# One-hots of a routing table moved to VectorE, more row tiles, and another order of expert passes

## The chip, the cores and the metric

The kernel runs on one core of a Trainium2 chip. The metric is the device time of one execution in microseconds (us); lower is better. Engines are called PE (TensorE, matrix products), PEld (its weight loads), DVE (VectorE), ACT (ScalarE), POOL (GpSimd) and SP (SyncE, which here only issues DMAs). Each engine works through its own queue in order.

## The reference

Two blocks follow each other, all in float32.

The first is a gated linear recurrence over 768 tokens, for 4 sequences of 8 heads with 48 channels. With f = sigmoid(f_logit), for each token

```
state = f[:, :, t, :, None] * state + k[:, :, t] (outer) v[:, :, t]
y[:, :, t] = q[:, :, t] @ state
```

The result, seen as 3072 tokens of 384 values, enters a mixture of experts. A token picks the best of 4 groups, then the best of 4 experts in that group (argmax of a softmax each), so that one of 16 experts works on it:

```
h = maximum(x @ w1[g, e], 0)        # 384 -> 1024
out[token] = g_w * e_w * (h @ w2[g, e])   # 1024 -> 384
```

An expert's two weight matrices are 1.5 MB each.

## The kernel before

**The recurrence stage.** Tokens are worked on in 6 chunks of 128, and a chunk in two halves of two sequences, which makes 12 units. Every unit passes through five stages, each one a generator: `gated`, `turned`, `scored`, `weighed`, `done`. In iteration i unit i is gated, unit i-1 turned, and so on. The text string `WEAVE` gives the order in which the generators of an iteration take one step each (a letter for a stage), and `LATE` does that for the last two iterations. On PE one unit is, in this order: `y` of the old state (L539), the logits `lT` (L574), `y` of the new scores (L544), scores `ap` (L523), the transpose `x_ps` (L582), `tr_q`/`tr_k` (L501), the state update `ds` (L554), `cs` (L479).

**Routing.** When both halves of a chunk are `done`, the generator `route` takes its 128x4 tokens through argmax (DVE), a rank within the expert (`rk`, two kinds of matmul, L191 and L194), a slot number `atf` (L207), weights, and last the table of slots: for each of the chunk's four groups of 128 tokens, `b`, POOL makes a one-hot `ln` of the slot's lane (L225) and a one-hot `val` of the slot's block times the two digits of the token's number (L228, two instructions). PE multiplies them into `tb` (L233, four matmuls that add up in one bank), and DVE adds that to `table` (L234). The letter `r` in the weave takes a step of it, only in iterations where the unit routed is the second half of its chunk; all of its steps stand in the last part of the iteration.

**Early experts.** After chunk 3 (`CLOSE`) `choose_early` takes the two fullest experts, loads their weights, and `early()` runs one block of 128 of their tokens each, in the last two iterations (letter `e`).

**The main stage.** `choose` ranks the experts by size and makes `who` (expert of each place) and `rows_p` (token numbers of each slot). Then come 16 passes, one for each place: the two early experts have a second block of 128, the others a width from `WIDTHS` (230 down to 174). A pass is: `fetch`, POOL's gather of token rows by indirect DMA (L355, one for 128 rows); `turn_in`, transposes (L368); `up` (L378); `down` (L404, or L397 for a block of 128, whose result is by token already); for the others `turn_out`, transposes back (L413); `put`, a scaling on DVE (L388) and a scatter by indirect DMA (L389). Row tiles of the early experts and of passes 0 and 1 come from a pool with two buffers; those of the other passes from one with four. Weights sit in three buffers: two in the pool `wp`, one in `wq`. Weights for pass n+3 are asked for after `down` of pass n.

**What sets the order.** The kernel is written with a framework that plans each engine's queue from the written order and from its own estimate of when operands and buffers are ready; a later instruction can be put ahead of one that it expects to be late. It adds all waits. At the end every engine reads two flags (L766) and branches over a slow path that isn't taken here.

Of the kernel before, what the change touches and what calls it, by code (L numbers as in the profile page):

```python
# [22 lines left out]
def kernel(  # L23
# [141 lines left out]
    def route(c, lg, sb, tabled=True):  # L165
# [53 lines left out]
        nc.sync.dma_start(out=rows_of(c)[:, :, DM:RW], in_=meta)  # L219
        yield  # L220
        if tabled:
            pairs = []
            for b in range(B):
                ln = tmp([P, P], "ln", BF16, bufs=4)
                nc.gpsimd.tensor_scalar(ln, lanes, atf[:, b, 0:1], None, OP.is_equal)  # L225
                val = tmp([P, 2, GE, 2], "val", BF16, bufs=4)
                for m in range(2):
                    nc.gpsimd.tensor_scalar(val[:, m], heads_of, atf[:, b, 1:2], part[:, c, b, m:m + 1], OP.is_equal, OP.mult)  # L228
                pairs.append((ln, val))
            yield  # L230
            tb = bank([P, 2, GE, 2], "tb")
            for b, (ln, val) in enumerate(pairs):
                nc.tensor.matmul(tb.rearrange("p m e j -> p (m e j)"), lhsT=ln, rhs=val.rearrange("p m e j -> p (m e j)"), start=(b == 0), stop=(b == B - 1))  # L233
            nc.vector.tensor_tensor(table, table, tb, OP.add)  # L234
        yield

# [113 lines left out]
    def fetch(pool, rows, n, top=N):  # L350

        w = {"n": n, "pool": pool, "blocks": [(j, min(P, n - j * P)) for j in range((n + P - 1) // P)]}
        w["x"] = pool.tile([P, len(w["blocks"]), RW], FP32, tag="xg", bufs=2 if pool is ep else 4, name="xg")
        for j, m in w["blocks"]:
            nc.gpsimd.indirect_dma_start(out=w["x"][0:m, j, :], out_offset=None, in_=x_dram[0:1 + top, :], in_offset=bass.IndirectOffsetOnAxis(ap=rows[0:m, j:j + 1], axis=0))  # L355
        return w
# [75 lines left out]
    with ExitStack() as fast:  # L432
# [132 lines left out]
        def done(i):  # L565
            c, s = units[i]
            xT = live[i]["xT"]
            if s == 0:
                groups[c] = sb.tile([P, B, NL], FP32, tag="lgs", name="lgs")

            lT = bank([P, P], "lT")
            for a in range(HP):
                for r in range(2):
                    nc.tensor.matmul(lT[DP * r:DP * r + DP, :], lhsT=gw[:, 2 * a + r].rearrange("p s l -> p (s l)"), rhs=xT[:, r, a, :], start=(a == 0), stop=(a == HP - 1), skip_group_check=True)  # L574
            lgT = sb.tile([P, P], FP32, tag="lgT", name="lgT")
            nc.scalar.copy(lgT, lT)
# [16 lines left out]
        def routed(i):  # L593

            c, s = units[i]
            if s:
                yield from route(c, groups[c], sb)
                if c == CLOSE:
                    choose_early(sb)
                    for p in range(EARLY):  # L600
                        weights[p] = load_weights(wp, who[0:1, p:p + 1])
                    first.append(early())
                    next(first[0])
                    yield

        first = []
        restart()
        WEAVE = "w d w s d t w d g s d t g r t r g r t r g r t r r".split()
        LATE = "w d w d d r e r d r e r e r r e r r e r e r".split()
        STAGES = (("g", gated), ("t", turned), ("s", scored), ("w", weighed), ("d", done), ("r", routed))  # L610
        LATER = dict(g=0, t=1, s=2, w=3, d=4, r=4)
        load(0)
        for i in range(NU + 4):
# [6 lines left out]
            gens = {nm: fn(i - LATER[nm]) for nm, fn in STAGES if 0 <= i - LATER[nm] < NU}  # L620
            for nm in WEAVE if i < NU + 2 else LATE:
                if nm in gens:
                    next(gens[nm], None)
                elif nm == "e":
                    next(first[0], None)

    with tc.tile_pool(name="cb", bufs=1) as cb:
        choose(cb)
# [2 lines left out]
    main = ctx.enter_context(ExitStack())  # L631
    wq = main.enter_context(tc.tile_pool(name="wq", bufs=1))
    mo = main.enter_context(tc.tile_pool(name="mo", bufs=2))
    NP = GE + EARLY

    def pass_of(n):

        if n < EARLY:
            return n, fetch(ep, rows_p[:, n, 1:2], P)
        p = n  # L640
        return p, fetch(mo, rows_p[:, p, :], WIDTHS[p - EARLY])

    fari = const([1, 1], I32, "fari")

# [11 lines left out]
    ws = {}  # L656
    for n in range(3):
        ws[n] = pass_of(n)[1]
    weights[2] = load_weights(wq, who[0:1, 2:3])
    for _ in first[0]:  # L660
        pass

    def run_up(n):
        for _ in up(ws[n], weights[n][0]):
            pass

    turn_in(ws[0])
# [1 line left out]
    turn_in(ws[1])  # L669
    for n in range(GE):  # L670
        if n + 3 < GE:
            ws[n + 3] = pass_of(n + 3)[1]
# [6 lines left out]
        down(ws[n], weights.pop(n)[1])  # L679
# [78 lines left out]
        beyond(True, sb)  # L758


    both = const([1, 2], I32, "both_i")
    rest = const([1, 1], I32, "rest")
    nc.vector.tensor_copy(both[:, 0:1], fari)
    nc.vector.tensor_scalar(rest, b_end, 0, None, OP.is_gt)
    nc.vector.tensor_tensor(both[:, 1:2], fari, rest, OP.max)
# [55 lines left out]
```

## Time and profile before

| what | value |
|---|---|
| median of 3 runs | 565.67 us (564.66 to 568.5) |
| profiled execution, its own time | 564.0 us |
| its span (first to last instruction) | 561.8 us |
| mean granted clock of PE | 0.91 of full |
| PE busy | 470.8 us, 84% of the span, 3855 instructions |
| DVE busy | 169.5 us, 30% |
| ACT busy | 115.8 us, 21% |
| POOL busy | 114.4 us, 20% |
| moved by DMA | 84.61 MB, 151 GB/s in the mean |

The profile is of one execution. Busy shares are means over stages that differ, so they say which engine does most, and not what a stage waits for. The recurrence stage lasts until about 241 us; the stretch to 265 us holds the choice of experts and the start of the main stage.

### The profile page before, as it was taken

The page shows a single profiled execution, that of the slowest core. Times are in us where ns is not written, and L with a number is a line of the kernel's source. Part 1 is how long each engine was busy: PE and PEld are TensorE (multiplying, and loading weights), DVE is VectorE, ACT ScalarE, POOL GpSimd, SP SyncE. Part 2 cuts the span into 40 slices and gives each one's busy share as a digit, 9 for nine tenths or more (in the row PEclk, how much of TensorE's full clock was granted, in tenths as well). Part 3 has the DMA queues.
Part 4 walks back from the last instruction along what each step waited for, and adds up shares of the span by engine and source line. Part 5 has one row for each costly group of instructions (what it writes and reads, how often), then busy time and mean ns, then how long its engine had stood idle before and what let it go on. Part 6 is the DMA issues. An engine that isn't in the chain of part 4 may idle for free. (4 is left out here: it accounts for less than half of the span.)

```text
span 561.8 us, 9341 instructions
## 1 busy us (share of the span) xinstructions
PE 470.8 (84%) x3855; PEld 422.7 (75%) x3855; DVE 169.5 (30%) x435; ACT 115.8 (21%) x245; POOL 114.4 (20%) x197
## 2 busy tenths in 40 slices
PE   2689689597795958781999999979999979999990
PEld 0468568386683847740988999979999879999990
DVE  4435626346155341363111122022111210221110
ACT  3466616255242211100100000101001000001000
POOL 5000130400404121246000012221222222122121
PEclk9789979689696877977899999999999998999996
DMA  9798746637201950138355257537655673574010
GB/s 192 122 212 192 158 91 153 131 83 158 45 29 30 345 190 29 30 116 247 127 194 208 94 225 257 169 112 262 220 174 175 240 255 86 194 256 154 7 38 24
DMA packets 138677, 84.61 MB, mean 151 GB/s; under 512 B 110629, under 2 KB 130131, under 8 KB 138627
## 3 DMA queue, kind: packets, MB, share of 16 engines
q1 hardware_dynamic: 132610, 74.07, 45.7%
q0 software_dynamic: 6016, 9.87, 5.7%
q8 instruction: 32, 0.52, 0.4%
q14 instruction: 19, 0.15, 0.1%
HBM read 74.38 MB, written 9.83 MB: 150 GB/s over the span
## 5 line engine op out<-in xcount | busy, mean ns | idle before, releaser
L378 PE MATMUL hp<-xe,w 128*128 128x128 f32 (+14 forms) x864 | 140.1, 323 | 1.6 <-DVE xe L369 1.6
L378 PEld LDWEIGHTS hp<-xe,w 128*128 128x128 f32 x864 | 137.0, 193 | 3.3 <-DVE xe L369 2.5
L404 PE MATMUL yo<-h,w 128*128 128x230 f32 (+13 forms) x672 | 118.5, 337 | 0.0
L404 PEld LDWEIGHTS yo<-h,w 128*128 128x128 f32 x672 | 114.7, 192 | 0.5
L389 POOL DMA_INDIRECT out_dram<-yt,xg x32 | 34.7, 1083 | 196.0 <-DVE yt L388 142.8
L380 DVE TENSOR_SCALAR h<-hp 128x256 f32<-128x256 f32 (+14 forms) x36 | 19.5, 541 | 146.9 <-PE hp L378 146.9
L225 POOL TENSOR_SCALAR ln<-lanes,atf 128x128 bf16<-128x128 f32 x24 | 14.4, 599 | 191.9 <-DVE atf L207 191.9
L382 ACT ACTIVATE h<-hp 128x256 f32<-128x256 f32 (+14 forms) x36 | 17.2, 478 | 140.7 <-PE hp L378 140.7
L525 DVE TENSOR_TENSOR am<-ap,tri 128x512 f32<-128x512 f32 x48 | 30.9, 684 | 43.4 <-PE ap L523 43.4
L355 POOL DMA_INDIRECT xg<-x_dram,rows_p x30 | 33.2, 1106 | 49.3 <-issue 36.0
L405 ACT COPY yT<-yo 128x230 f32<-128x230 f32 (+13 forms) x28 | 9.1, 326 | 156.3 <-PE yo L404 156.3
L479 PE MATMUL cs<-ld_f,tri 128*128 128x384 f32 x48 | 23.0, 570 | 15.6 <-ACT ld_f L473 15.6
L233 PE MATMUL tb<-val,ln 128*128 128x64 bf16 x24 | 5.1, 211 | 36.3 <-POOL val L228 36.3
L368 PE MATMUL xg_ps<-ident,xg 128*128 128x128 f32 (+14 forms) x96 | 13.5, 264 | 19.0 <-DMA xg<-x_dram,rows_p 18.8
L539 PEld LDWEIGHTS y<-Tq,st 48*64 48x64 f32 x320 | 16.4, 174 | 16.2 <-issue 16.1
L523 PE MATMUL ap<-Tq,Tk 48*128 48x128 f32 x384 | 28.2, 287 | 0.0
L544 PE MATMUL y<-am,v 128*64 128x128 f32 x384 | 27.1, 302 | 0.0
L368 PEld LDWEIGHTS xg_ps<-ident,xg 128*128 128x128 f32 (+14 forms) x96 | 10.4, 143 | 22.0 <-issue 11.9
L523 PEld LDWEIGHTS ap<-Tq,Tk 48*128 48x128 f32 x384 | 23.6, 190 | 4.1 <-issue 3.9
L544 PEld LDWEIGHTS y<-am,v 128*64 128x64 f32 x384 | 25.9, 158 | 0.0
L539 PE MATMUL y<-Tq,st 48*64 48x128 f32 x320 | 25.6, 352 | 0.0
L405 DVE COPY yT<-yo 128x230 f32<-128x230 f32 (+13 forms) x14 | 5.1, 366 | 67.8 <-issue 35.4
(160 smaller groups left out, 485.0 us busy)
## 6 DMA issues: line engine op xcount, KB each, us to landing
w<-in_moe_w_dram SPq DMA_DIRECT2D x32, 1536.0 KB
ld_f<-in_f_logit_dram SPq DMA_DIRECT2D x12, 384.0 KB
ld_k<-in_k_dram SPq DMA_DIRECT2D x12, 384.0 KB
qh<-in_q_dram SPq DMA_DIRECT2D x12, 384.0 KB
v<-in_v_dram SPq DMA_DIRECT2D x12, 384.0 KB
x_dram<-x SPq DMA_DIRECT2D x12, 384.0 KB
out_dram<-yt,xg POOLq DMA_INDIRECT x32, 3.7
xg<-x_dram,rows_p POOLq DMA_INDIRECT x30, 6.7
```

The source lines that it names most:

```text
L355: nc.gpsimd.indirect_dma_start(out=w["x"][0:m, j, :], out_offset=None, in_=x_dram[0:1 + top, :], in_offset=bass.IndirectOffsetOnAxis(ap=ro ...
L368: nc.tensor.transpose(out=pt[:, ko, 0:m], in_=w["x"][0:m, j, ko * P:(ko + 1) * P], identity=ident[0:m, 0:m])
L378: nc.tensor.matmul(hp[:, o, :], lhsT=w1[:, ko, (f + o) * P:(f + o + 1) * P], rhs=w["xT"][:, ko, :], start=(ko == 0), stop=(ko == KO - 1))
L380: nc.vector.tensor_scalar(h[:, f:f + 2, :], hp, 0.0, None, OP.max)
L382: nc.scalar.activation(h[:, f:f + 2, :], hp, AF.Relu)
L389: nc.gpsimd.indirect_dma_start(out=out, out_offset=bass.IndirectOffsetOnAxis(ap=w["x"][0:m, j, DM + 1:RW].bitcast(U32), axis=0), in_=y[0:m ...
L404: nc.tensor.matmul(yp, lhsT=w2[:, fo, m * P:(m + 1) * P], rhs=w["h"][:, fo, :], start=(fo == 0), stop=(fo == FO - 1))
L479: nc.tensor.matmul(cs.rearrange("t h d -> t (h d)"), lhsT=tri, rhs=nl[:, b], start=True, stop=True)
L523: nc.tensor.matmul(ap[r][:, a, :], lhsT=w["Tk"][rows, b, a, :], rhs=w["Tq"][rows, b, a, :], start=True, stop=True)
L525: nc.vector.tensor_tensor(am[:, r], ap[r], tri.unsqueeze(1).broadcast_to((P, HP, P)), OP.mult)
L539: nc.tensor.matmul(ys[r][DP * b:DP * b + DP, a, :], lhsT=old[rows, b, a, :], rhs=w["Tq"][rows, b, a, :], start=(a == 0), stop=False, skip_ ...
L544: nc.tensor.matmul(ys[r][DP * b:DP * b + DP, a, :], lhsT=w["v"][:, b, 2 * a + r, :], rhs=w["am"][b][:, r, a, :], start=(c == 0 and a == 0) ...
```

## The change

It has five parts.

1. In `route`, the one-hots are made by DVE. One operation makes `ln` for all four groups of 128 tokens (512 columns); `head` (128 columns) is the one-hot of the block, and two products make `val`. A step more stands between them, so that `route` has seven steps with a table.
2. `route` is no longer tied to a unit: when the second half of a chunk has its logits, its generator joins a list, and each `r` of the weave takes a step of the first in the list. `r` stands five times in `WEAVE`, beginning right after the step that makes the logits, so that a chunk's routing runs on into the next iteration.
3. The row tiles `xg` of the main stage have six buffers instead of four.
4. The order of passes is 0, 2, 3, ..., 15, 1: the second block of the second early expert comes last. Its weights were loaded for the early block, and are loaded once more for the last pass, so that there are 34 weight DMAs instead of 32. Weights of the next two places are asked for at the start of the main stage.
5. `LATE` holds ten `e` in its two iterations instead of fourteen, which leaves the last step of `early()`, the `down` of the second early expert, behind `choose`. The flags for the end are computed in the main stage.

```diff
         if tabled:
-            pairs = []
+            ln = tmp([P, B, P], "ln", BF16)
+            nc.vector.tensor_tensor(ln, lanes.unsqueeze(1).broadcast_to((P, B, P)), atf[:, :, 0:1].broadcast_to((P, B, P)), OP.is_equal)
+            yield
+            BLK = (P, B, 2 * GE)
+            head = tmp(list(BLK), "head")
+            nc.vector.tensor_tensor(head, heads_of.rearrange("p e j -> p (e j)").unsqueeze(1).broadcast_to(BLK), atf[:, :, 1:2].broadcast_to(BLK), OP.is_equal)
+            val = tmp([P, 2, B, 2 * GE], "val", BF16)
+            for m in range(2):
+                nc.vector.tensor_tensor(val[:, m], head, part[:, c, :, m:m + 1].broadcast_to(BLK), OP.mult)
+            yield
+            tb = bank([P, 2, GE, 2], "tb")
             for b in range(B):
-                ln = tmp([P, P], "ln", BF16, bufs=4)
-                nc.gpsimd.tensor_scalar(ln, lanes, atf[:, b, 0:1], None, OP.is_equal)
-                val = tmp([P, 2, GE, 2], "val", BF16, bufs=4)
-                for m in range(2):
-                    nc.gpsimd.tensor_scalar(val[:, m], heads_of, atf[:, b, 1:2], part[:, c, b, m:m + 1], OP.is_equal, OP.mult)
-                pairs.append((ln, val))
-            yield
-            tb = bank([P, 2, GE, 2], "tb")
-            for b, (ln, val) in enumerate(pairs):
-                nc.tensor.matmul(tb.rearrange("p m e j -> p (m e j)"), lhsT=ln, rhs=val.rearrange("p m e j -> p (m e j)"), start=(b == 0), stop=(b == B - 1))
+                nc.tensor.matmul(tb.rearrange("p m e j -> p m (e j)"), lhsT=ln[:, b], rhs=val[:, :, b, :], start=(b == 0), stop=(b == B - 1))
             nc.vector.tensor_tensor(table, table, tb, OP.add)
...
-        w["x"] = pool.tile([P, len(w["blocks"]), RW], FP32, tag="xg", bufs=2 if pool is ep else 4, name="xg")
+        w["x"] = pool.tile([P, len(w["blocks"]), RW], FP32, tag="xg", bufs=2 if pool is ep else 6, name="xg")
...
+                    if s:
+                        routes.append(routed(c))
...
-        WEAVE = "w d w s d t w d g s d t g r t r g r t r g r t r r".split()
-        LATE = "w d w d d r e r d r e r e r e r r e r r e r e r".split()
+        WEAVE = "w d w s d r t w d g s d r t g r t r g t r g t".split()
+        LATE = "w d w d r w d r d e r r e r e r r r e r r e".split()
...
-    NP = GE + EARLY
+    PLACES = [0] + list(range(EARLY, GE)) + list(range(1, EARLY))
...
+    def flags():
+
+        nc.vector.tensor_copy(both[:, 0:1], fari)
+        nc.vector.tensor_scalar(rest, b_end, 0, None, OP.is_gt)
+        nc.vector.tensor_tensor(both[:, 1:2], fari, rest, OP.max)
...
-    weights[2] = load_weights(wq, who[0:1, 2:3])
+    ahead = {n: load_weights(wq if n % 3 == 1 else wp, who[0:1, PLACES[n]:PLACES[n] + 1]) for n in range(1, 2)}
+    ahead[0] = weights[0]
...
+        if n == 0:
+            ahead[2] = load_weights(wp, who[0:1, PLACES[2]:PLACES[2] + 1])
...
-            weights[n + 3] = load_weights(wq if n % 3 == 2 else wp, who[0:1, n + 3:n + 4])
+            ahead[n + 3] = load_weights(wq if n % 3 == 1 else wp, who[0:1, PLACES[n + 3]:PLACES[n + 3] + 1])
...
         if n == 3:
             weakest()
+            flags()
```

## Rows read from the trace of the kernel before

**Rows 1.** The page: busy tenths in 40 slices of 14.05 us, and PE's clock.

```profile
PE   2689689597795958781999999979999979999990
PEclk9789979689696877977899999999999998999996
```

**Rows 2.** Waits of PE: us in total, times, longest us.

```profile
PE tb L233 <- POOL val L228: 36.3, 24, 5.1
PE xg_ps L368 <- DMA xg<-x_dram,rows_p: 18.8, 7, 11.1
PE rk L191 <- DVE ohe L186: 3.0, 2, 2.4
```

**Rows 3.** Timeline of PE: start us, us, instruction, count, idle time before it.

```profile
58.58 0.66 PE L582 MATMUL x_ps<-ident,xT 128*128 128x128 f32 x4
...
81.52 0.66 PE L582 MATMUL x_ps<-ident,xT 128*128 128x128 f32 x4
...
93.45 0.66 PE L582 MATMUL x_ps<-ident,xT 128*128 128x128 f32 x4
...
104.90 0.21 PE L233 MATMUL tb<-val,ln 128*128 128x64 bf16 x1 [4.37 <-POOL val L228]
...
117.54 0.66 PE L582 MATMUL x_ps<-ident,xT 128*128 128x128 f32 x4
```

**Rows 4.** Stretches: length, busy PE, PEld, DVE, ACT, POOL, clock, DMA, GB/s.

```profile
66.00:84.00 18.00, 11.72 (x144) 9.53 (x145) 5.18 (x16) 4.00 (x8) 6.09 (x13) 0.72 0.46 89
100.00:118.00 18.00, 11.68 (x110) 9.47 (x109) 4.08 (x15) 4.27 (x9) 6.07 (x13) 0.62 0.43 83
...
35.00:65.00 30.00, 30.00 (x434) 25.31 (x431) 18.25 (x39) 19.18 (x39) 0.00 (x0) 1.00 0.94 200
```

**Rows 5.** Timelines of DVE (first three) and POOL (last two), one chunk's routing.

```profile
96.31 0.23 DVE L176 TENSOR_TENSOR dl<-lgs,mx 128x80 f32<-128x80 f32 x1
...
97.94 1.28 DVE L525 TENSOR_TENSOR am<-ap,tri 128x512 f32<-128x512 f32 x2
...
103.00 0.17 DVE L207 CAST atf<-at 128x8 f32<-128x8 int32 x1
...
206.85 0.61 POOL L225 TENSOR_SCALAR ln<-lanes,atf 128x128 bf16<-128x128 f32 x1 [21.44 <-DVE atf L207]
207.46 0.92 POOL L228 TENSOR_SCALAR val<-heads_of,atf,part 128x32 bf16<-128x32 f32 x2
```

**Rows 6.** Timeline of all engines, from the last chunk's slots to pass 0.

```profile
234.88 0.17 DVE L207 CAST atf<-at 128x8 f32<-128x8 int32 x1
...
241.22 0.21 PE L233 MATMUL tb<-val,ln 128*128 128x64 bf16 x1 [1.27 <-POOL val L228]
...
246.58 0.16 DVE L291 CAST rows_p<-got 128x32 uint32<-128x32 f32 x1
...
250.34 1.04 POOL L389 DMA_INDIRECT out_dram<-yt,xg  x1 [0.30 <-DVE more L315]
...
258.96 0.96 POOL L355 DMA_INDIRECT xg<-x_dram,rows_p  x1 [0.31 <-issue]
...
265.23 0.87 PE L368 MATMUL xg_ps<-ident,xg 128*128 128x128 f32 x3 [11.11 <-DMA xg<-x_dram,rows_p]
```

**Rows 7.** PE's wait between 266 and 548 us; then two stretches, as in group 4.

```profile
PE xg_ps L368 <- DMA xg<-x_dram,rows_p: 7.7, 6, 3.3
...
300.00:540.00 240.00, 232.13 (x1402) 228.06 (x1401) 42.84 (x93) 21.54 (x52) 48.60 (x45) 0.99 0.53 179
247.00:261.00 14.00, 7.12 (x23) 3.85 (x21) 7.45 (x17) 0.00 (x0) 10.97 (x9) 0.95 0.95 301
```

**Rows 8.** Timeline: `down` of a block of 128, and the last two scatters.

```profile
280.82 5.35 PE L397 MATMUL yo<-w,h 128*128 128x384 f32 x16
...
549.24 1.00 POOL L389 DMA_INDIRECT out_dram<-yt,xg  x1 [2.35 <-DVE yt L388]
...
553.11 1.17 POOL L389 DMA_INDIRECT out_dram<-yt,xg  x1 [2.86 <-DVEq L767]
```

More of the change, by code (lines that the diff above doesn't have):

```diff
@@ L221, in route @@
         if tabled:
-            pairs = []
-            for b in range(B):
-                ln = tmp([P, P], "ln", BF16, bufs=4)
-                nc.gpsimd.tensor_scalar(ln, lanes, atf[:, b, 0:1], None, OP.is_equal)
-                val = tmp([P, 2, GE, 2], "val", BF16, bufs=4)
-                for m in range(2):
-                    nc.gpsimd.tensor_scalar(val[:, m], heads_of, atf[:, b, 1:2], part[:, c, b, m:m + 1], OP.is_equal, OP.mult)
-                pairs.append((ln, val))
+            ln = tmp([P, B, P], "ln", BF16)
[7 more added lines that the diff above has]
+                nc.vector.tensor_tensor(val[:, m], head, part[:, c, :, m:m + 1].broadcast_to(BLK), OP.mult)
             yield
             tb = bank([P, 2, GE, 2], "tb")
-            for b, (ln, val) in enumerate(pairs):
-                nc.tensor.matmul(tb.rearrange("p m e j -> p (m e j)"), lhsT=ln, rhs=val.rearrange("p m e j -> p (m e j)"), start=(b == 0), stop=(b == B - 1))
+            for b in range(B):
+                nc.tensor.matmul(tb.rearrange("p m e j -> p m (e j)"), lhsT=ln[:, b], rhs=val[:, :, b, :], start=(b == 0), stop=(b == B - 1))
             nc.vector.tensor_tensor(table, table, tb, OP.add)
@@ L591, in done, with routed, advance @@
             yield
[L593 to L603, printed above, removed]
-                    yield
-        first = []
+        def routed(c):
+            yield from route(c, groups[c], sb)
+            if c == CLOSE:
+                choose_early(sb)
+                for p in range(EARLY):
+                    weights[p] = load_weights(wp, who[0:1, p:p + 1])
+                first.append(early())
+                next(first[0])
+                yield
+        def advance(gens):
+            if gens and next(gens[0], True):
+                gens.pop(0)
+        first, routes = [], []
         restart()
-        WEAVE = "w d w s d t w d g s d t g r t r g r t r g r t r r".split()
-        LATE = "w d w d d r e r d r e r e r r e r r e r e r".split()
-        STAGES = (("g", gated), ("t", turned), ("s", scored), ("w", weighed), ("d", done), ("r", routed))
-        LATER = dict(g=0, t=1, s=2, w=3, d=4, r=4)
+        WEAVE = "w d w s d r t w d g s d r t g r t r g t r g t".split()
+        LATE = "w d w d r w d r d e r r e r e r r r e r r e".split()
+        STAGES = (("g", gated), ("t", turned), ("s", scored), ("w", weighed), ("d", done))
         load(0)
-        for i in range(NU + 4):
+        for i in range(NU + len(STAGES) - 1):
             if i + 1 < NU:
@@ L619 @@
                 nc.sync.dma_start(out=x_dram[0:1, DM:RW], in_=blank[:, D:D + 2])
-            gens = {nm: fn(i - LATER[nm]) for nm, fn in STAGES if 0 <= i - LATER[nm] < NU}
+            gens = {nm: fn(i - late) for late, (nm, fn) in enumerate(STAGES) if 0 <= i - late < NU}
             for nm in WEAVE if i < NU + 2 else LATE:
-                if nm in gens:
-                    next(gens[nm], None)
+                if nm == "r":
+                    advance(routes)
                 elif nm == "e":
                     next(first[0], None)
+                elif nm in gens:
+                    next(gens[nm], None)
+        while routes:
+            advance(routes)
     with tc.tile_pool(name="cb", bufs=1) as cb:
@@ L633 @@
     mo = main.enter_context(tc.tile_pool(name="mo", bufs=2))
-    NP = GE + EARLY
+    PLACES = [0] + list(range(EARLY, GE)) + list(range(1, EARLY))
     def pass_of(n):
[L638 to L641, printed above, removed]
+        p = PLACES[n]
+        if p < EARLY:
+            return fetch(mo, rows_p[:, p, 1:2], P)
+        return fetch(mo, rows_p[:, p, :], WIDTHS[p - EARLY])
     fari = const([1, 1], I32, "fari")
@@ L654, in weakest @@
         nc.vector.tensor_copy(fari, far[:, 1:2])
-    ws = {}
-    for n in range(3):
-        ws[n] = pass_of(n)[1]
-    weights[2] = load_weights(wq, who[0:1, 2:3])
+    def flags():
+        nc.vector.tensor_copy(both[:, 0:1], fari)
+        nc.vector.tensor_scalar(rest, b_end, 0, None, OP.is_gt)
+        nc.vector.tensor_tensor(both[:, 1:2], fari, rest, OP.max)
+    both = const([1, 2], I32, "both_i")
+    rest = const([1, 1], I32, "rest")
+    ws = {n: pass_of(n) for n in range(3)}
+    ahead = {n: load_weights(wq if n % 3 == 1 else wp, who[0:1, PLACES[n]:PLACES[n] + 1]) for n in range(1, 2)}
+    ahead[0] = weights[0]
     for _ in first[0]:
@@ L663, in run_up @@
     def run_up(n):
-        for _ in up(ws[n], weights[n][0]):
+        for _ in up(ws[n], ahead[n][0]):
             pass
@@ L671 @@
         if n + 3 < GE:
-            ws[n + 3] = pass_of(n + 3)[1]
+            ws[n + 3] = pass_of(n + 3)
+        if n == 0:
+            ahead[2] = load_weights(wp, who[0:1, PLACES[2]:PLACES[2] + 1])
         if n + 1 < GE:
@@ L678 @@
             turn_in(ws[n + 2])
-        down(ws[n], weights.pop(n)[1])
+        down(ws[n], ahead.pop(n)[1])
         if n + 3 < GE:
-            weights[n + 3] = load_weights(wq if n % 3 == 2 else wp, who[0:1, n + 3:n + 4])
+            ahead[n + 3] = load_weights(wq if n % 3 == 1 else wp, who[0:1, PLACES[n + 3]:PLACES[n + 3] + 1])
         if n == 2:
@@ L758, in scan @@
         beyond(True, sb)
[L761 to L765, printed above, removed]
     more = nc.values_load(both[0:1, 1:2], min_val=0, max_val=1, skip_runtime_bounds_check_because="the result of a comparison")
```

## Prediction

> **What bounds the kernel now.** I read the two lines of the page first [rows 1]: PE's digits are mostly 9 in the second half and change between 5 and 9 in the first, with a 1 in the slice that begins at 253 us, and the clock's digits sink to 6 and 7 where PE's do. So PE is the bound in the main stage, and in the recurrence something stops it again and again. Which wait that is stands in PE's waits [rows 2]: of all that PE waits for, `tb` on POOL's `val` is the most, 36.3 us in 24 waits. 24 is four matmuls in each of six chunks, 6.05 us a chunk. In order of time [rows 3], one sees what a chunk pays. The transposes `x_ps` mark the same place of each unit. From 81.52 to 93.45 is 11.93 us, a unit without routing; from 93.45 to 117.54 is 24.09 us, a unit with `tb`. From 58.58 to 81.52, the chunk before, is 22.94. Taking off 0.3 us for the matmuls of routing, the unit with `tb` loses 11.9 and 10.7 us, about twice the idle time. The other half is PE's clock [rows 4]: in the 18 us from 66 the granted clock is 0.72 of full, in those from 100 it is 0.62, which is 10 and 14 us at the lower of the two levels (1.2 instead of 2.4 GHz). PE had stood still before it fell both times. From 35 to 65, where PE never stands still, the clock is 1.00, and PE is busy 30.00 of 30.00 us with DVE at 18.25 and ACT at 19.18: at that pace the other engines and the loads (DMA share 0.94) keep up. Five of the six chunks lie in the recurrence; two have a clock like the first stretch, three like the second.
>
> **Table one-hots.** Removed: 24 `ln` of 0.61 us and 48 `val` of 0.46 us on POOL, (0.61+0.92) x 4 = 6.1 us a chunk [rows 5]. Added on DVE, a chunk: `ln` with 512 columns, whose nearest row is the masking with 512 columns, 0.64 us; `head` and two `val` with 128 columns, between the 0.23 us of 80 columns and that 0.64. I take 0.25 each, near the smaller shape, so 0.64 + 0.75 = 1.4 us, bounds 1.3 to 2.6. On DVE, with 18.25 of 30 us busy, this lies beside PE's work. Queued behind it on DVE are the masking of scores and the scaling of q and k, which PE reads some us later.
>
> What does `tb` wait for then? In the trace `atf` ends at 103.17 [rows 5], while PE arrived at `tb` at 104.90 - 4.37 = 100.5 [rows 3]: 2.7 us of the first wait is DVE's being late, and a faster one-hot alone wouldn't remove it. The weave does: the step with `tb` is now the second `r` of the next iteration, behind that iteration's scores, and by the letters PE has about two thirds of a unit, 8 of 11.93 us, more to do before it. PE would arrive at about 108.5, and DVE is done at 103.17 + 1.4 = 104.6 plus what else is in its queue. So the wait goes. Late next is `rk`, which waits for `ohe` by the same chain: 3.0 us in all now [rows 2], and its step comes somewhat earlier. I leave 3.0 us more for it, over all chunks. With the steps move the small DMA of `meta` on SP and POOL's copy for it; what is queued behind it on SP are loads for later units. Early experts are chosen half a unit later, 6 us, while their weights take 20 to 28 us at the rate of [rows 7]. If either comes late, that is the second rival. What the recurrence gains: 2 x 10.7 + 3 x 11.9 = 57, less 3, is **54 us**; with no new wait 57, with `rk` standing still and the clock falling at every chunk far less (below).
>
> **A rule about the clock.** The rows give about half of those 57 us to the clock: 57 - 5 x 6.05 = 27. The Trainium skill, TensorE: Matmul & The Clock Gate, Part 1, says that for modelling the loss while the clock comes up is under 1% of a typical kernel's span. By that figure an estimate of the clock's part is at most 5.6 us, and the forecast would be some 21 us higher. The rows speak against it here.
>
> **From the last chunk to pass 0** [rows 6]. `atf` ends at 235.05, the last `tb` starts at 241.22, `rows_p` is made at 246.58, the scatter of the first early block goes out at 250.34, the gather for pass 0 at 258.96, and PE's transposes follow at 265.23, when that gather has landed, after 11.11 us of idle PE. The one-hots now take 1.4 us instead of six, so `tb` ends at about 237.4 and all behind it is 3.8 us earlier. The gather for pass 0 needs the buffer of the early block just scattered, and in the trace it stands behind six other gathers on POOL, about 1.3 us each. With six buffers, four more gathers could be planned ahead of it: 5 us later; if it goes out as soon as its buffer is free, 6 us earlier. The `down` of the second early block now lies behind `choose`; in the trace both already ran there, so this is worth nothing. Gain between -1 and 10, taken as **4 us**, the plain shift.
>
> **Weights.** One expert more is loaded (3.1 MB). From 247 to 261 us the DMA engines run at a share of 0.95 and move 301 GB/s [rows 7]: one expert is 10 to 14 us. In the main stage the share is 0.53 over 240 us, so there the load is hidden by PE's work; without that cover it costs up to 14. Pass 0 alone, instead of 0 and 1, must now cover the weights of the third place. Those are on their way while the rows are chosen and are there by 261 us, before pass 0 begins: nothing. The load for the next place needs a buffer of the early experts.
>
> **Row tiles.** Between 266 and 548 us PE waits 7.7 us in six waits for gathers [rows 7], because a gather with four buffers goes out only once an earlier pass is scattered. With six it can go out two passes earlier. Gain 0 to 7.7; I take **7**. Scatters stand in the same POOL queue, and the earlier gathers are issued between them: about 1.3 us for each, while POOL is busy 48.60 of 240 us.
>
> **Last pass.** Before, two scatters close the kernel, the second 3.87 us behind the first, since it waits for that one [rows 8]; the span ends 8.7 us after the second starts. A block by token needs one scatter and no transposes back, but it still waits for the two of the pass before, which have only its `down` of 5.35 us as cover. Gain 0 to 3.9; I take **2**. The flags are three tiny DVE operations that move, beside PE's work: nothing.
>
> **Sum.** 54 + 4 + 7 + 2 = 67 us. The profiled execution took 564.0 us (span 561.8, 2.2 around it), 1.7 below the median of 565.67. 564 - 67 = 497, and on the median's scale **498 us**.
>
> **The rivals.**
> - *`tb` stays where it is.* The plan needn't follow the letters; if it puts `tb` at the end of the unit, PE arrives at 100.5, the one-hots are ready at 104.6, and PE waits 4.1 instead of 6.05 us, with the clock falling as now. Six chunks gain 2 each, 12, and with the other 13 that makes 541 us. For it: the late `atf`. Against: PE's order in the trace is the weave's, letter by letter. Chance 0.09, of which 0.02 that the smaller gains fail too and it stays within 1%.
> - *Loads become late at the faster pace, or the main stage starts hungry.* The loads keep the DMA engines at 0.94 in the stretch from 35 to 65, and the pace there would now last. A unit late by 2 us in six units is 12 us, an expert's weights late at the start about as much: 510. Chance 0.10.
> - *The clock's half doesn't come back*, as it would if the low stretches weren't caused by the stop before them: 498 + 27 = 525. The two kinds of stretch in [rows 4] say no. Chance 0.04. This is where the page's figure belongs; by it 519.
> - *Slower: two waits in place of one.* `rk` and `tb` now come at different places, each behind a DVE chain in its own half of a unit. If PE stands still at both, for 4.1 us each and with the clock falling after each (the 5.4 us of a chunk above), a chunk pays 2 x 9.5 = 19 instead of 11.4, 38 us in five, less 13 from the rest: 590. It decides from a sum of both waits and their clock of 14 us a chunk. Against it: `rk` waited in two chunks only. Chance 0.03.
>
> **Numbers.** The forecast has 0.74, and the time is its own. Its own ends: 57 instead of 54, 10 instead of 4, and 7.7 and 3.9 at the end give 486.5; nothing from the last three and 6 us less in the recurrence give 517. The range of 484 to 522 holds it and the hungry loads, and leaves out the other rivals, 0.16. A measurement of this kernel tells about 1%, 5.7 us, from no change. Faster by more than that: 0.74 + 0.07 + 0.10 + 0.04 = 0.95; within it 0.02; slower 0.03.
>
> **What will show it.** In the changed kernel's profile PE's wait `tb` on POOL is gone, and none on DVE of more than 1 us a chunk takes its place; `x_ps` to `x_ps` is 12 us in each unit from the third to the tenth; the clock line has 9 from slice 3 to the choice of experts; the idle time before pass 0's transposes is still there, 5 to 13 us long; PE's waits for gathers in the main stage are below 2 us; the last scatter starts less than 5 us after PE's last matmul. I am wrong if PE waits at `tb` or `rk` for DVE in every chunk, if units without any wait of PE are longer than 12.5 us, or if PE waits for weights.

## The result and the profile after

The changed kernel takes **479.1 us** in the median of four runs (479.03 to 484.37), the kernel before 565.16 (563.65 to 568.5): a ratio of 0.8493, with an interval of 0.8424 to 0.8562. The forecast was 498, with a range of 484 to 522. The direction and the main mechanism were right; the time lies 5 us below the range. One step of the forecast, named below, is worth more than the whole difference; the other terms were a little too hopeful together.

The span went from 561.8 to 477.0 us, 84.8 less. Four marks of the two timelines split it: the start of the last unit's logits `lg`, the start of pass 0's transposes `xg_ps`, the end of PE's last matmul, the end of the span.

| stretch | before, us | after, us | gained | forecast |
|---|---|---|---|---|
| start to the last `lg` | 230.2 | 174.4 | 55.9 | 54 |
| last `lg` to pass 0's transposes | 35.0 | 19.6 | 15.4 | 4 |
| pass 0 to PE's last matmul | 283.0 | 270.2 | 12.8 | 7 |
| from there to the end | 13.6 | 12.8 | 0.8 | 2 |

The first two rows are not quite like for like. With fewer `e` in `LATE`, 48 of the 96 `up` matmuls of the early blocks stand ahead of the last `lg` and not 60, as PE's timelines show (the kernel before, then the changed one):

```profile
221.67 6.96 PE L378 MATMUL hp<-xe,w 128*128 128x128 f32 x60 [0.32 <-DVE xe L369]
```

```profile
167.18 5.60 PE L379 MATMUL hp<-xe,w 128*128 128x128 f32 x48 [0.37 <-issue]
```

The twelve that moved take 1.4 us; with them in one place the recurrence gains 54.5 and the second stretch 16.8.

The page of the changed kernel, which answers to [rows 1] (a slice is now 11.9 us); its last line is the count of weight loads:

```profile
span 477.0 us, 9296 instructions
...
PE   1679999999999799799999999999999999999990
...
PEclk9989999999999899999999999999999999999995
...
w<-in_moe_w_dram SPq DMA_DIRECT2D x34, 1536.0 KB
```

Counting slices from 0, PE is at 9 from slice 3 up to the last but for two slices of 7, and the clock is too, but for one 8 at the first of these two. The waits of PE (us in all, times, longest), against [rows 2]:

```profile
PE cs L480 <- ACT ld_f L474: 15.6, 3, 10.3
PE rk L191 <- DVE ohe L186: 3.3, 3, 2.4
...
PE hp L379 <- DVE xe L370: 1.4, 2, 0.8
PE xg_ps L369 <- DMA w<-in_moe_w_dram: 1.4, 1, 1.4
PE tb L234 <- DVE val L230: 0.5, 1, 0.5
```

The first row lies in the first 40 us and was there before. Of the 36.3 us at `tb` 0.5 is left, of the 18.8 us at `xg_ps` 1.4, and `rk` is as it was. The timeline of PE, against [rows 3] and the last row of [rows 6]:

```profile
70.56 0.66 PE L583 MATMUL x_ps<-ident,xT 128*128 128x128 f32 x4
...
74.51 0.29 PE L234 MATMUL tb<-val,ln 128*128 128x64 bf16 x4
82.61 0.66 PE L583 MATMUL x_ps<-ident,xT 128*128 128x128 f32 x4
...
95.25 0.66 PE L583 MATMUL x_ps<-ident,xT 128*128 128x128 f32 x4
...
158.95 0.20 PE L191 MATMUL rk<-ohe,strictb 128*128 128x64 bf16 x1 [2.37 <-DVE ohe L186]
...
180.54 0.29 PE L234 MATMUL tb<-val,ln 128*128 128x64 bf16 x4 [0.53 <-DVE val L230]
...
193.98 0.52 PE L369 MATMUL xg_ps<-ident,xg 128*128 128x128 f32 x3 [1.40 <-DMA w<-in_moe_w_dram]
```

From `x_ps` to `x_ps` it is 12.05 us with a `tb` between them and 12.64 with an `rk` that waits 0.57 us, where [rows 3] had 24.09 and 11.93. The four `tb` follow one another in 0.29 us without a wait. Before pass 0 PE stands still for 1.40 us, not 11.11. The profile puts that wait down to a load of weights, and the forecast had called it a sign of being wrong if PE waits for weights. The transposes read only rows and `ident`; by the trace's semaphore events the gather of the rows landed at 193.78 us and that load at 193.80, so the gather alone would have held PE about as long. Three stretches, columns as in [rows 4]: the recurrence, the start of the main stage, the rest of it.

```profile
56.00:160.00 104.00, 101.06 (x1571) 86.34 (x1571) 74.05 (x224) 57.41 (x119) 3.27 (x6) 1.00 0.69 172
...
186.00:206.00 20.00, 17.18 (x98) 13.70 (x97) 10.30 (x26) 1.32 (x3) 14.11 (x13) 1.00 0.94 308
206.00:464.00 258.00, 258.00 (x1572) 251.36 (x1570) 48.38 (x105) 23.50 (x57) 51.04 (x48) 1.00 0.57 196
```

The clock is 1.00 where [rows 4] had 0.72 and 0.62, with DVE busy 71% of the time. From 206 us on PE has no idle time at all, where [rows 7] had 7.7 us of waits. DVE's one-hots in the last chunk, and the rows of the passes:

```profile
178.66 0.17 DVE L207 CAST atf<-at 128x8 f32<-128x8 int32 x1
...
179.08 0.68 DVE L223 TENSOR_TENSOR ln<-lanes,atf 128x512 bf16<-128x512 f32 x1
179.68 0.28 DVE L227 TENSOR_TENSOR head<-heads_of,atf 128x128 f32<-128x128 f32 x1
179.99 0.49 DVE L230 TENSOR_TENSOR val<-head,part 128x128 bf16<-128x128 f32 x2
...
186.22 0.16 DVE L292 CAST rows_p<-got 128x32 uint32<-128x32 f32 x1
```

They take 1.45 us a chunk; the forecast had 1.4. POOL, from pass 0's gather to the scatter of the first early block, and the last two scatters:

```profile
187.30 0.96 POOL L356 DMA_INDIRECT xg<-x_dram,rows_p  x1 [34.89 <-DVE more L316]
...
192.87 1.02 POOL L390 DMA_INDIRECT out_dram<-yt,xg  x1 [0.30 <-DVE minb L335]
...
463.69 1.18 POOL L390 DMA_INDIRECT out_dram<-yt,xg  x1 [2.85 <-DMA out_dram<-yt,xg]
468.59 1.00 POOL L390 DMA_INDIRECT out_dram<-yt,xg  x1 [3.72 <-DVEq L781]
```

This is the row that the forecast had the other way round. In [rows 6] the scatter goes out first and pass 0's gather 8.6 us after it. Now the gather is the first thing POOL does once the rows are known, 1.1 us after `rows_p`, and 5.6 us ahead of the scatter. It waits for no buffer. The reason is a line of the change that the shortened diff above does not show and that I did not weigh:

```diff
         if p < EARLY:
-            return n, fetch(ep, rows_p[:, n, 1:2], P)
+            return fetch(mo, rows_p[:, p, 1:2], P)
```

The rows of passes 0 and 1 are no longer put into the pool `ep` of the early blocks, with its two buffers, but into `mo`, the main stage's own. The pool also gives these passes their other work tiles; the wait that the traces show is the gather's.

### The profile page after: what moved, and what is told of

It reads as the page before. It is cut to its first block, busy times and chain, and to the rows that moved or that the text cites. A ratio compares the mean times of both kernels' runs of the same rounds, so it can differ in the third digit from the quotient of the medians.

```text
span 477.0 us, 9296 instructions
## 1 busy us (share of the span) xinstructions
PE 439.9 (92%) x3855; PEld 402.5 (84%) x3855; DVE 175.2 (37%) x459; ACT 116.0 (24%) x245; POOL 78.4 (16%) x125
## 5 line engine op out<-in xcount | busy, mean ns | idle before, releaser
L405 PE MATMUL yo<-h,w 128*128 128x230 f32 (+13 forms) x672 | 116.8, 334 | 0.0
L405 PEld LDWEIGHTS yo<-h,w 128*128 128x128 f32 x672 | 113.0, 190 | 0.5
L545 PE MATMUL y<-am,v 128*64 128x128 f32 x384 | 23.7, 276 | 0.0
L480 PEld LDWEIGHTS cs<-ld_f,tri 128*128 128x128 f32 x48 | 8.6, 220 | 16.8 <-issue 10.9
L545 PEld LDWEIGHTS y<-am,v 128*64 128x64 f32 x384 | 22.0, 139 | 0.1
L398 PE MATMUL yo<-w,h 128*128 128x384 f32 x64 | 21.2, 487 | 0.0
L489 DVE TENSOR_TENSOR qh<-qh,eq 128x768 f32<-128x768 f32 x12 | 11.5, 957 | 26.0 <-ACT eq L481 26.0
L218 POOL COPY meta<-token 128x4 int32<-128x4 int32 x6 | 1.9, 320 | 108.0 <-DVE kh L491 59.4
L398 PEld LDWEIGHTS yo<-w,h 128*128 128x128 f32 x64 | 11.9, 190 | 7.7
L502 PE MATMUL tr_q<-ident,qh 128*128 128x128 f32 x96 | 16.4, 297 | 1.7 <-DVE qh L489 1.7
```

The source lines that it names most:

```text
L398: nc.tensor.matmul(yp, lhsT=w["h"][:, fo, :], rhs=w2[:, fo, :], start=(fo == 0), stop=(fo == FO - 1))
L405: nc.tensor.matmul(yp, lhsT=w2[:, fo, m * P:(m + 1) * P], rhs=w["h"][:, fo, :], start=(fo == 0), stop=(fo == FO - 1))
L480: nc.tensor.matmul(cs.rearrange("t h d -> t (h d)"), lhsT=tri, rhs=nl[:, b], start=True, stop=True)
L502: nc.tensor.transpose(out=pt[:, a, :], in_=w[nm + "h"][:, b, 2 * a:2 * a + 2, :].rearrange("t r d -> t (r d)"), identity=ident)
L545: nc.tensor.matmul(ys[r][DP * b:DP * b + DP, a, :], lhsT=w["v"][:, b, 2 * a + r, :], rhs=w["am"][b][:, r, a, :], start=(c == 0 and a == 0) ...
```

## The experiments

In the accounts below "gap" is PE's idle time before pass 0's transposes. All medians stand beside the kernel before on the same chip, 563.9 to 566.2 us. The changed kernel's 479.1 us, from which differences are taken, became 478.9 and 482.5 us when it ran again on two of the chips, so a difference of 3 us between chips tells little.

**Pass 0 back in the early pool.** The changed kernel with that one line taken back. This is the kernel that the forecast describes.

```diff
         if p < EARLY:
-            return fetch(mo, rows_p[:, p, 1:2], P)
+            return fetch(ep, rows_p[:, p, 1:2], P)
```

> The changed kernel with one line put back: the token rows of pass 0 and of the last pass go into the two-buffer pool of the early blocks again, so that pass 0's gather has to wait until an early block is scattered. Theory A (that line is what the forecast of the start of the main stage missed): the gather for pass 0 falls back behind four or more others on GpSimd, PE stands still 8 to 12 us before pass 0 instead of 1.4, the clock falls after it, and the kernel takes 488 to 493 us. Theory B (the gap closed because the one-hots are earlier and PE's clock stays up): within 2 us of 479.

499.78 us (497.77 to 500.25), ratio 0.8832 (0.8795 to 0.8868). The line is worth 20.7 us of the gain; the forecast's 498 is inside the spread of this kernel's runs. POOL's timeline:

```profile
193.47 1.02 POOL L390 DMA_INDIRECT out_dram<-yt,xg  x1 [0.31 <-issue]
...
199.07 0.94 POOL L356 DMA_INDIRECT xg<-x_dram,rows_p  x1 [0.30 <-issue]
204.91 0.97 POOL L356 DMA_INDIRECT xg<-x_dram,rows_p  x1 [4.89 <-DMA out_dram<-yt,xg]
```

and PE's:

```profile
211.80 0.88 PE L369 MATMUL xg_ps<-ident,xg 128*128 128x128 f32 x3 [19.11 <-DMA xg<-x_dram,rows_p]
...
213.32 8.28 PE L379 MATMUL hp<-xe,w 128*128 128x128 f32 x48 [0.65 <-DVE xe L370]
```

Pass 0's gather stands behind eight others and then waits until the scatter that frees its buffer has landed, 10.4 us after POOL had issued it. The gap is 19.11 us, more than I had expected of it, and the 48 matmuls of the first `up` behind it take 8.28 us instead of 5.62; the granted clock is 0.65 from 211.8 to 222 us.

**The same line alone, in the kernel before.**

```diff
-            return n, fetch(ep, rows_p[:, n, 1:2], P)
+            return n, fetch(mo, rows_p[:, n, 1:2], P)
```

> The kernel before with one edit: the rows of passes 0 and 1 go into the main stage's row tiles, so that pass 0's gather waits for no scatter. Routing, weave and all else as before. Theory A (the wait for a buffer made the idle time before pass 0): PE stands still 0 to 4 us there instead of 11, the clock falls less, and the kernel takes 548 to 556 us. Theory B (the gather was held up by the weights on the DMA engines): 561 us or more.

552.04 us (550.91 to 553.03), ratio 0.9782 (0.975 to 0.9814): 11.8 us. PE's waits show the gap of 11.11 us gone and the rest nearly as in [rows 2]:

```profile
PE tb L233 <- POOL val L228: 36.4, 24, 5.1
...
PE xg_ps L368 <- DMA xg<-x_dram,rows_p: 7.5, 5, 3.7
```

So the line is worth about the gap that it removes: 11 us here, 18 of 19 in the changed kernel.

**The one-hots on DVE, alone.** The kernel before, with `ln`, `head` and `val` on DVE in one step, and the old weave.

```diff
-                ln = tmp([P, P], "ln", BF16, bufs=4)
-                nc.gpsimd.tensor_scalar(ln, lanes, atf[:, b, 0:1], None, OP.is_equal)
...
+            ln = tmp([P, B, P], "ln", BF16)
+            nc.vector.tensor_tensor(ln, lanes.unsqueeze(1).broadcast_to((P, B, P)), atf[:, :, 0:1].broadcast_to((P, B, P)), OP.is_equal)
```

> The kernel before, with the one-hots made by DVE (four operations for a chunk, in one step), everything else as before: routing tied to its unit, the old weave, the old main stage. Theory A (the place of tb decides, the engine of the one-hots little): PE reaches tb while DVE is still busy, waits about 4 us in one wait instead of 6 in four, the clock still falls after it, and the kernel takes 535 to 545 us. Theory B (the one-hots on GpSimd were the whole wait): PE's wait at tb is under 1 us a chunk, and the kernel takes 500 to 510 us. Theory C (the wait stays at 4 us and the clock doesn't fall for so short a wait): 515 to 528 us.

535.42 us (534.27 to 537.77), ratio 0.9481 (0.9437 to 0.9525). PE's waits (first), then a row of DVE's timeline and one of PE's:

```profile
PE tb L233 <- DVE val L229: 21.5, 6, 4.7
```

```profile
98.72 0.17 DVE L207 CAST atf<-at 128x8 f32<-128x8 int32 x1
...
100.41 0.39 PE L233 MATMUL tb<-val,ln 128*128 128x64 bf16 x4 [4.16 <-DVE val L229]
```

Each of the first five chunks still stops PE, once for 3.2 to 4.7 us instead of four times. It is the first wait of [rows 3], 4.37 us, almost unchanged: a producer that is 4.7 us faster cures the three short waits and not the long one. PE arrives at 96.25 and `atf` ends at 98.89, so 2.6 us of the wait are `atf`'s; the other 1.5 are the one-hots of all four groups on DVE, which take as long as POOL's for the first group alone, 0.61 + 0.92 us [rows 5]. Two stretches around such stops, columns as in [rows 4]:

```profile
96.00:108.00 12.00, 7.84 (x106) 6.90 (x105) 5.17 (x17) 4.09 (x8) 0.30 (x1) 0.72 0.54 101
126.00:138.00 12.00, 7.26 (x105) 6.44 (x104) 5.80 (x20) 4.09 (x9) 0.37 (x1) 0.72 0.55 102
```

0.72 over 12 us is 6.7 us at 1.2 GHz, where [rows 4] had 10 and 14.

**The weave alone.** The changed kernel with its one-hots back on POOL; `tb` stays at its new place.

```diff
-            ln = tmp([P, B, P], "ln", BF16)
-            nc.vector.tensor_tensor(ln, lanes.unsqueeze(1).broadcast_to((P, B, P)), atf[:, :, 0:1].broadcast_to((P, B, P)), OP.is_equal)
...
+            pairs = []
+            for b in range(B):
+                ln = tmp([P, P], "ln", BF16, bufs=4)
+                nc.gpsimd.tensor_scalar(ln, lanes, atf[:, b, 0:1], None, OP.is_equal)
```

> The changed kernel, with the one-hots made by GpSimd again as before the change (three instructions for each of the four groups of 128 tokens); the new weave, the list of routes and tb's later place stay. Theory A (the place of tb decides): GpSimd's 6 us lie between atf and tb's later place, PE waits 0 to 2 us a chunk in the five chunks of the recurrence and some 4 us at the last chunk, and the kernel takes 481 to 492 us. Theory B (the engine decides): PE waits 4 to 6 us at each tb and the clock falls, 525 us or more.

487.96 us (486.32 to 488.64), ratio 0.8638 (0.8607 to 0.867), 8.9 us above the changed kernel. PE's timeline, a `tb` of the recurrence and the last chunk's:

```profile
98.94 0.29 PE L234 MATMUL tb<-val,ln 128*128 128x64 bf16 x4
...
181.78 0.19 PE L234 MATMUL tb<-val,ln 128*128 128x64 bf16 x1 [0.61 <-POOL val L228]
183.26 0.19 PE L234 MATMUL tb<-val,ln 128*128 128x64 bf16 x1 [1.29 <-POOL val L228]
...
186.22 0.19 PE L234 MATMUL tb<-val,ln 128*128 128x64 bf16 x1 [1.29 <-POOL val L228]
```

With POOL's six microseconds a chunk unchanged PE waits 0.2 us at most in each of the first four chunks, and 1.16 in the fifth. In the recurrence the new weave, with `tb`'s place, gives all but 1.2 us of the gain with the slow engine left in: the last `lg` starts at 175.5 us, against 174.4. The faster engine counts in the last chunk, where nothing is left to put ahead of `tb`.

**All of routing, with the old main stage.** The kernel before with parts 1, 2 and the new `LATE`.

```diff
-        w["x"] = pool.tile([P, len(w["blocks"]), RW], FP32, tag="xg", bufs=2 if pool is ep else 6, name="xg")
+        w["x"] = pool.tile([P, len(w["blocks"]), RW], FP32, tag="xg", bufs=2 if pool is ep else 4, name="xg")
...
-    PLACES = [0] + list(range(EARLY, GE)) + list(range(1, EARLY))
+    NP = GE + EARLY
```

> The kernel before with the whole routing part of the change (one-hots on DVE, list of routes, both weaves) and the main stage as before: four row tiles, passes in their old order, rows of passes 0 and 1 in the early pool. Theory A: the recurrence gains its 56 us, the stretch to pass 0 only what the earlier table gives, about 6, and the kernel takes 500 to 505 us, so that the main stage's part of the change is worth 21 to 26. Theory B (the main stage's part is worth what was forecast, 9 us): 488 us.

505.68 us (504.08 to 507.02), ratio 0.8939 (0.8903 to 0.8974). That is just above the range of theory A. The main stage's part of the change is thus 26.6 us, not 9. Its waits keep both terms; below them are pass 0's gather on POOL and the transposes on PE:

```profile
PE xg_ps L369 <- DMA xg<-x_dram,rows_p: 22.7, 6, 14.4
```

```profile
203.04 0.97 POOL L356 DMA_INDIRECT xg<-x_dram,rows_p  x1 [3.94 <-DMA out_dram<-yt,xg]
...
206.19 0.88 PE L369 MATMUL xg_ps<-ident,xg 128*128 128x128 f32 x3 [14.43 <-DMA xg<-x_dram,rows_p]
```

14.4 is the gap, the other 8.3 lie between the passes.

**Four row tiles.** The changed kernel with `bufs=4` in place of 6.

> The changed kernel with four row tiles in the main stage instead of six. Theory A (tiles hold the gathers back): PE's waits for gathers in the main stage come back, 6 to 9 us with a dip of the clock after the longest, and the kernel takes 485 to 490 us. Theory B (in the new order gathers go out early enough anyway): within 2 us of 479.

493.26 us (492.06 to 495.9), ratio 0.8748 (0.8722 to 0.8775), above what I had expected. PE's waits:

```profile
PE xg_ps L369 <- DMA xg<-x_dram,rows_p: 11.0, 6, 5.6
```

Two tiles are worth 14.2 us here, not 7: 11.0 us of waits and some of the clock behind the longest. Why the waits are 11.0 us and not the 8.3 of routing alone, the runs don't show; the two kernels differ in the pool of passes 0 and 1 and in the order of passes. The terms are not additive: the line is worth 20.7 us beside the tiles, the tiles 14.2 beside the line, and the whole main stage 26.6.

**The old order of passes.** The changed kernel with the passes in order, both early weights kept, one load fewer.

```diff
-    PLACES = [0] + list(range(EARLY, GE)) + list(range(1, EARLY))
+    PLACES = list(range(GE))
...
-    ahead[0] = weights[0]
+    ahead = {0: weights[0], 1: weights[1], 2: load_weights(wq, who[0:1, 2:3])}
```

> The changed kernel with the passes in their old order, 0, 1, 2, ..., 15, both early experts' weights kept for it, so that one load of 3.1 MB fewer is made and the last pass is one of 174 rows with two scatters. Rows of passes 0 and 1 stay in the main pool. Theory A (the order is worth the tail only): 480 to 483 us. Theory B (the load made twice costs time at the start of the main stage, and the order loses what it wins): 476 to 479 us.

478.32 us (477.78 to 479.53), ratio 0.8484 (0.8461 to 0.8508): no difference that can be told from the changed kernel's 479.1. Pass 0 to PE's last matmul takes 270.3 us against 270.2, and from there to the end it is 13.20 us against 12.83. The block by token as last pass, and the load that it costs, are worth nothing together.

**The rank of the fifth chunk later.** The one long wait left in the recurrence is the 2.37 us at `rk`. One iteration gets a weave of its own that puts `rk` behind more of PE's work.

```diff
-            for nm in WEAVE if i < NU + 2 else LATE:
+            for nm in "w d w s d r w d s d r".split() if i == NU + 1 else WEAVE if i < NU + 2 else LATE:
```

> The changed kernel with another weave for one iteration (the last before LATE): two steps of routing instead of five, so that the rank of the fifth chunk comes behind the next unit's matmuls. Theory A (PE's stop of 2.37 us at rk and the dip of the clock after it are the last loss of the recurrence): both go, and the kernel takes 474 to 477 us. Theory B (the time comes back as a later choice of the experts): within 1 us of 479.

475.97 us (475.86 to 479.12), ratio 0.8453 (0.8425 to 0.8481). Then together with the old order of passes, and, on the same chip, the changed kernel once more:

> The two kernels that beat or equalled the changed one, put together: passes in their old order with both early experts' weights kept, and the rank of the fifth chunk one iteration later. Theory A (they touch different stretches, so they add up): 474 to 476 us. Theory B (the gain of the later rank is lost where the early experts begin): 478 us or more.

> The changed kernel itself once more, on the same chip as the run beside it, for the comparison: 478 to 480 us.

479.48 us (478.92 to 480.89), ratio 0.8499 (0.8481 to 0.8516), and 482.53 (479.89 to 485.42), ratio 0.8533 (0.851 to 0.8556). Both were some 3 us slower than expected; the later rank seemed not to add up, until the pair is compared with itself: 3.05 us apart, though the two differ in the order of passes as well and their runs overlap. What both have and the earlier runs don't is a stop at the second pass's `up`. The changed kernel's repeat, DVE and PE:

```profile
195.77 5.62 PE L379 MATMUL hp<-xe,w 128*128 128x128 f32 x48 [0.65 <-DVE xe L370]
...
203.36 0.42 DVE L381 TENSOR_SCALAR h<-hp 128x256 f32<-128x256 f32 x1 [4.19 <-PE xg_ps L369]
...
205.36 6.91 PE L379 MATMUL hp<-xe,w 128*128 128x230 f32 x19 [3.38 <-issue]
```

and the same two in the first profile of the changed kernel:

```profile
195.15 5.62 PE L379 MATMUL hp<-xe,w 128*128 128x128 f32 x48 [0.65 <-DVE xe L370]
...
200.81 0.43 DVE L381 TENSOR_SCALAR h<-hp 128x256 f32<-128x256 f32 x1 [2.25 <-PE hp L379]
...
202.13 9.59 PE L379 MATMUL hp<-xe,w 128*128 128x230 f32 x48 [0.77 <-DVE xe L370]
```

The repeat is 0.6 us late at the first `up` and 3.2 us at the second. By the records the first `up` ends at 201.39, and DVE's `h`, which reads its product, starts 2.0 us after that; in the other profile it starts at once, 200.81 after 200.77. The ends of matmuls in the records are modelled, while the semaphore that PE raises behind them is recorded. In the repeat it is raised for this product at 203.34 us, 0.02 ahead of `h`, and for the two groups of transposes behind it at 203.39 and 204.81, whose records end at 201.72 and 201.99; in the other profile the first two come 0.01 us behind the records' ends. So it is PE that was late, and DVE took up the product at once. The profile names no cause ("issue"). The repeat's last row above stops where its view does, at 212 us; the whole 48 matmuls take 12.54 us instead of 9.59, at a granted clock of 0.75 from 205 to 218 us. To settle the later rank, both versions ran side by side once more:

> The changed kernel as it is, now on the same chip as the kernel with the last rank later, since the two have only been compared over different chips (479.1 and 482.5 against 476.0 us). Theory A (the later rank is worth what PE's 2.37 us of waiting and the 1.7 us of low clock behind it cost): 478 to 483 us, and 2 to 4 us above the other kernel of this job. Theory B (the 3 us were the chip's): within 1 us of the other kernel. On the start of the main stage: theory C (what stops PE at the second pass's up is chance, in any version): a wait of 0.6 to 3.5 us there in the profile; theory D (only certain chips): as the other kernel's in this job.

> The changed kernel with the last chunk's rank one step of the weave later, once more, beside the changed kernel. Theory A: 474 to 480 us, 2 to 4 us below the changed kernel of this job, no wait at rk over 0.7 us in the profile. Theory B: within 1 us of it. A wait of 2 us or more at the second pass's up would take the gain back in the runs that have it.

478.88 us (478.65 to 479.9), ratio 0.8475 (0.8454 to 0.8496), and **475.76** (475.4 to 476.72), ratio 0.8417 (0.8396 to 0.8438): 3.1 us, with runs that do not overlap. PE's timeline of the second:

```profile
161.37 0.20 PE L191 MATMUL rk<-ohe,strictb 128*128 128x64 bf16 x1
...
165.75 0.29 PE L234 MATMUL tb<-val,ln 128*128 128x64 bf16 x4 [0.86 <-DVE val L230]
```

`rk` waits no more, `tb` 0.86 us, and the granted clock from 150 to 180 us is 1.00 instead of 0.94. This pair differs in the weave alone, and the pair before it gave about the same 3 us; this is the fastest version found, by 0.6% of the time. The stop of 2.2 us and more at the second pass's `up` was seen on one chip of the three used for the experiments, in the one profile of each of the two versions that ran there.

## Why the prediction was right in kind and 19 us too high

**The step that failed** is the sentence "The gather for pass 0 needs the buffer of the early block just scattered", in the part from the last chunk to pass 0. It is true of the kernel before and was carried over to the changed one past a line of the diff that ends it. With it the stretch was bounded to a gain of -1 to 10 us and taken as 4; it gained 15.4, and the statement that 5 to 13 us of idle time would still stand before pass 0 was wrong by the same step (1.40). The first experiment prices it: with that one line put back the kernel takes 499.8 us, 20.7 more, of which 17.7 lie in this stretch and 3.0 in the next, where the first `up` then runs at the lower clock. The forecast was 19 us too high, so all other terms together were some 2 us too hopeful.

**Within that kernel**, the one that the forecast describes, the agreement with 498 is in part luck, since two errors cancel. From the last `lg` to pass 0 it takes 37.3 us, 2.3 more than before, where I had taken 4 less and at worst 1 more. Pass 0 to PE's last matmul gains 9.8 us, where 7 had been taken. Between routing alone and this kernel, which differ by the tiles, the order of passes and the last pass, the gap grows from 14.43 to 19.11. These are not the "four more gathers" of the prediction, planned ahead of pass 0's: eight stand ahead of it in both kernels, six in the kernel before. Of the 4.7 us, 3.7 are the gather's own way, 6.9 us from its start on POOL to PE's transposes (204.91 to 211.80) instead of 3.2 (203.04 to 206.19). Why it takes longer stays open; three more gathers are issued right behind it there. In the same step pass 0 to PE's last matmul falls from 285.8 to 273.2. Net, the medians are 5.9 us apart, where tiles and last pass had been put at 9.

**Recurrence, 54.** Right: 55.9, or 54.5 without the early matmuls that moved. The parts are less exact than the sum. The waits at `tb` of the first five chunks, 31.8 us, are gone, where five times 6.05 had been counted; the clock gave back 23, where 27 had been counted; and `rk` costs 0.6 us more, not 3. That `tb` would follow the letters of the weave was the weak point, with a rival of its own at 541. The weave-alone kernel shows that the letters, not the engine, carry this term. The one-hots-alone kernel shows that PE would otherwise have stood still for 3.2 to 4.7 us in each of the five chunks, as that rival had it, but also that the rival was priced too low: it gained 30 us, not 12, for the most part because the clock, which the rival left as it was, fell for less long (6.7 us at a stop instead of 10 and 14).

**The clock.** The rows said that half of what a chunk loses is the clock's, and most of that came back: 1.00 over the stretch from 56 to 160 us. Up to the last `lg` PE is busy for 178.2 us before and 153.8 after; 1.4 of the difference are the moved matmuls, so 23 us are the clock's, 4% of the span before. The Trainium skill, TensorE: Matmul & The Clock Gate, Part 1, puts the loss while the clock comes up at under 1% of a typical kernel's span, which as an estimate is at most 5.6 us here. It says so of a kernel's warm-up, and this trace does not agree for a kernel that is stopped once a chunk, since the clock fell and came up again at each stop; the 23 us measured decide.

**One-hots on DVE, 1.4 us a chunk.** Right, 1.45. No wait of PE for DVE grew by more than 0.6 us.

**Row tiles, 7.** Right in kind, all six waits are gone, and too small, because the term left the clock out. The stretch gained 12.8 us: 7.7 of waits, and 5.1 by which PE's busy time fell (273.8 to 268.8 us) for the same matmuls. Of these, 1.4 are the first `up` (7.04 us before, 5.62 after) and belong to the gap before pass 0. With passes 0 and 1 in the same pool the two tiles are worth 14.2.

**Last pass, 2, and the extra load, 0.** The last scatter starts 4.4 us after PE's last matmul, as stated, and the end gained 0.8. The order of passes as a whole gave nothing.

**The rivals.** `tb` did not stay where it was; no load was late in the recurrence (PE is busy 101 of 104 us at a DMA share of 0.69); the clock came back; two waits in place of one did not come, the rank's 2.37 us being an old one. Only the hungry start showed, in small: PE waits 0.7 to 1.0 us at the second pass's `up` in most profiles, 2.2 and 3.4 in two, not 12.

**What stays open:** what holds PE at the end of the first `up` and in the transposes behind it on that chip. Its semaphores come late there, and no row says why.

## What to carry to other kernels

A wait of an in-order engine has a place and a producer: before speeding the producer up, see how much of the wait is already there when the producer starts, since moving the waiting instruction behind other work cured four chunks of five with the slow producer left in. Where a transfer is forecast to wait, look up which pool its buffer comes from in the kernel as changed, line by line; a one-word change of pool was worth 12 to 21 us here. Terms that meet at the same buffers do not add: without that line, the rest of the main stage's change lengthened the wait before pass 0 from 14.4 to 19.1 us.

## What was not expected of the hardware

- In the first experiment a scatter that POOL had issued by 194.5 us freed its buffer only 10.4 us later, while weights and eight gathers were under way or being issued at the start of the main stage.
- One stop of 4.2 us went with 6.7 us at the lower clock, the four stops of a chunk before, 6 us in all [rows 2], with 10 and 14 us [rows 4]. Half of such a time is lost, so the clock costs 3.4 us in the one and 5 to 7 in the other, somewhat less than the wait or about as much. After the stop of 2.37 us at `rk` in the changed kernel, which ends at 158.95, the granted clock is 0.50 from 160 to 162 us.
- On one chip PE raised the semaphore of a finished group of matmuls 1.9 us, and of the transposes behind it 1.7 and 2.8 us, after the ends that the records give them, at a DMA share of 0.96 between 186 and 206 us; in the changed kernel's first profile, at 0.94, the first two came 0.01 us after.
